# Softmax steps, rstd, weight conversion and the last batch's theta and y rearranged in a fused attention and gating kernel

## The chip, the cores and the metric

The kernel runs on one core of one Trainium2 chip. The metric is the device time of one execution in microseconds (us), as the median of several runs. The engines are named as in the profile: PE (TensorE matmul), PEld (its weight load), DVE (VectorE), ACT (ScalarE), POOL (GpSimd) and SP (SyncE, which here issues every DMA).

## What is computed

Attention with two kinds of masks (4 local heads, 4 strided heads), then a gated layer with a normalization and a mixing over tokens, then a layer with cos and sin of theta and a second mixing over tokens. B = 4, S = 576, 8 heads of 64, so d = 512. Cut to what matters:

```python
scores = where(mask, 0.125 * q @ k.T, -1e9); attn = softmax(scores)   # + 1e-9 in the divisor
x = merge_heads(attn @ v)                                   # (4, 576, 512)
h = relu(x @ w_in); u, v = h[..., :512], h[..., 512:]
v_n = (v - mean(v)) / sqrt(var(v) + 1e-6)
x2 = (u * (einsum('ts,bsd->btd', w_spatial, v_n) + b_spatial)) @ w_out
theta = x2 @ w_theta
y = einsum(w_tok_r, x2 * cos(theta)) + einsum(w_tok_i, x2 * sin(theta))
t = x2 + y
out = t + relu(t @ w_ch)
```

The weights w_in, w_out, w_theta, w_tok_r, w_tok_i and w_ch arrive as float64.

## The kernel before

Every large matmul takes a value as a pair of float16 tensors, hi and lo, and is done in three passes (`PASS`: hi·hi, lo·hi, hi·lo), each as two matmuls of 288 columns (`mm2`). The hi part is a copy (ACT as a rule), the lo part a subtraction on DVE or POOL.

**Order of the work.** Generators for the main path (`main_v`, `main_mid`, `main_end`) yield after each chunk; at each yield `others()` hands out conversion parts whose due time has come (by a count of matmul columns, `clock`) and steps of the attention of a later batch (`ATT_AT`). The Tile scheduler then sets each engine's order from priorities; `hv`, `ha` and `hg` issue with a priority raised by `AHEAD`. Each engine works its list in order. For a batch the main path is v (with the statistics and `rstd`), then u and sp (the first mixing), x (w_out), th (theta, with `z_chunk` for cos and sin), then y (the second mixing) and c (w_ch). y and c of batch b come after v of batch b+1, so that other matmuls lie between th and y; the last batch has no v behind it, and y follows th at once.

**Attention.** Batches 0 and 1 run in float32 (`attention32`, L408), 11 units each. A unit goes: scores on PE into a PSUM tile, a maximum on DVE (L395), the step that multiplies it by -0.125 (L403, DVE, 96x4 or 128x4), four Exp with sums on ACT (L405), then in `softmax_div` a step on the sums (L341, DVE), a reciprocal (L342) and a multiplication (L343); then a transpose on PE (L445), its copy out (L446, ACT), the matmul with v (L420), and the evacuation of `av` into xT (L355 on ACT, L356 on DVE). Batches 2 and 3 (`attention`, L485) use float16 pairs and the same `softmax_div` with another scale. In batch 1, `sc` and `av` have one PSUM buffer each, so that the PE waits at L445 for the evacuation L356 of an earlier unit.

**Conversion of float64 weights** (`stage`, `from_f64`, `part`, `prep_w`, `tok_part`; L189 to L258). A block of 128 rows and 512 or 576 columns is loaded as raw 64 bit words, scaled in place on ACT (L203), put together with three integer operations on DVE (L204, L205, L206), copied to float16 on ACT (L119) and subtracted on POOL (L211). There are 29 such blocks: 8 of w_in, 4 of w_out, 4 of w_theta, 9 of the token weights, 4 of w_ch. Until `switch`, the raw words lie in the two halves of `x2f` in turn and the values in quarters of `x2h`; after it, in tiles of the pools `s2` and `s1`. `WIN_AT` sets after which units of the first attention a w_in block is handed out, `CONV_*` hold due time, lead and gap of the others.

**rstd** (L527) is a chain of 15 small DVE steps on 128x5, with the copy at L592: a shift estimate and three Newton rounds.

**The end.** In `main_mid` (L694) th of column blocks 0 and 1 is done for rows 0 to 2 of x2h first, block 0 then block 1, and then row 3 of each; blocks 2 and 3 follow whole. A `z_chunk` (L673) is a chain over ACT and DVE: turns (ACT, `ta<-th`), fraction (DVE), Abs and two Sin (ACT), a product with x2f (DVE), the hi copy into vn (ACT), the lo subtraction (DVE), and then two DMA transposes from vn into zf (L686, hi and lo), after which y can use the block. `main_end` (L707) runs y of a column block over 9 row groups, in each of them the three passes.

Of the kernel before, what the change touches and what calls it, by code (L numbers as in the profile page):

```python
# [13 lines left out]
F32 = mybir.dt.float32  # L14
# [37 lines left out]
E_ZLO = 'vvvvvvvv'  # L52
WARM = 6
ATT_AT = (None, (2.7, 4.0), (74.5, 4.4), (169.9, 4.6))
WIN_AT = (0, 0, 0, 0, 1, 1, 1, 1)
CONV_SP = (20.0, 9.9, 1.9)
CONV_OUT = (37.0, 12.0, 2.5)
CONV_TH = (49.0, 12.0, 2.5)
CONV_TOK = (61.0, 10.0, 2.0)
CONV_CH = (87.0, 14.1, 2.4)  # L60
F64_SHIFT = 2.0 ** -111


# [1 line left out]
def kernel(  # L65
# [118 lines left out]

    early = [True, 0]

    xs4 = [x2h[:, e, c:c + 2, :].rearrange("p c n -> p (c n)").bitcast(F32)[:, 0:S] for e in range(2) for c in (0, 2)]

    def stage():  # L189
        if early[0]:  # L190
            i = early[1]
            early[1] += 1
            return x2f[:, i % 2 * 2:i % 2 * 2 + 2, :].rearrange("p a n -> p (a n)").bitcast(I64), xs4[i % 4]
        return s2("wstg").rearrange("p a n -> p (a n)").bitcast(I64), s1("wx")
# [18 lines left out]
    def prep_w(dst_hi, dst_lo, src, n, late=True):  # L213
        stg, x = stage()
        nc.sync.dma_start(stg[:, 0:n], src)
        part(dst_hi, dst_lo, from_f64(stg, x, n), late)

    def win_parts(half):
        c = slice(half * DM, (half + 1) * DM)
        for i in range(NC):  # L220
            yield lambda i=i: prep_w(win[:, 0, i, c], win[:, 1, i, c], w_in[i * P:(i + 1) * P, c], DM, False)

    def sq_parts(dst, src):
        for i in range(NC):
            yield lambda i=i: prep_w(dst[:, 0, i, :], dst[:, 1, i, :], src[i * P:(i + 1) * P, :], DM)

    def sp_part(i):
        stg = stage()[0].bitcast(F32).rearrange("p (a n) -> p a n", a=2)
        nc.sync.dma_start(stg, w_spT[i * P:(i + 2) * P, :].rearrange("(a p) n -> p a n", p=P))
        nc.scalar.activation(wsp[:, 0, i:i + 2, :], stg, AF.Copy, scale=SPS)  # L230
        nc.vector.scalar_tensor_tensor(wsp[:, 1, i:i + 2, :], stg, SPS, wsp[:, 0, i:i + 2, :],
                                       op0=ALU.mult, op1=ALU.subtract)

    def sp_tail():
        stg = stage()[0].bitcast(F32).rearrange("p (a n) -> p a n", a=2)
# [12 lines left out]
    def tok_part(i):  # L248

        stg, x = stage()  # L250
        r = 0
        while r < P:
            g = i * P + r
            w, k = (w_tr, g) if g < S else (w_ti, g - S)
            n = min(P - r, S - k)
            nc.sync.dma_start(stg[r:r + n, 0:S], w[k:k + n, :])
            r += n
        part(wtok[:, 0, i, :], wtok[:, 1, i, :], from_f64(stg, x, S), True)  # L258


    SOFF = [0, 126, 252, 378, 448]
# [130 lines left out]
    def softmax32(sc, sm, st, R, way):  # L392
        X = mybir.AxisListType.X
        mx = st[0:R, 0, :]
        nc.vector.tensor_reduce(out=mx.rearrange("p (i j) -> p i j", i=2), in_=sc[0:R], op=ALU.max, axis=X)  # L395
        smv = sm[0:R].rearrange("p (i j) k -> p i j k", i=2)
        if way == "d":
            nc.vector.tensor_tensor(smv, sc[0:R], mx.rearrange("p (i j) -> p i j", i=2).unsqueeze(3).broadcast_to(
                [R, 2, 2, P]), ALU.subtract)
            nc.scalar.activation(sm[0:R], sm[0:R], AF.Exp, scale=0.125)  # L400
            nc.vector.tensor_reduce(out=st[0:R, 2, :], in_=sm[0:R], op=ALU.add, axis=X)
        else:
            nc.vector.tensor_scalar(st[0:R, 1, :], mx, -0.125, None, op0=ALU.mult)  # L403
# [123 lines left out]
    def rstd(st, n, rows):  # L527
        r = slice(0, rows)
        a, y, t = st[r, 0, 0:n], st[r, 1, 0:n], st[r, 2, 0:n]
        hv.tensor_scalar(a, a, 1e-6, None, op0=ALU.add)  # L530
        hv.tensor_scalar(t.bitcast(I32), a.bitcast(I32), 1, None, op0=ALU.logical_shift_right)
        hv.tensor_scalar(y.bitcast(I32), t.bitcast(I32), -1, 0x5F3759DF, op0=ALU.mult, op1=ALU.add)
        hv.tensor_scalar(a, a, -0.5, None, op0=ALU.mult)
# [21 lines left out]
    def main_v(b):  # L555
# [25 lines left out]
        for pr in V_ORDER:  # L581
# [31 lines left out]
    def main_mid(b):  # L613
# [93 lines left out]
    def main_end(b):  # L707
# [17 lines left out]

# [36 lines left out]
    timed([lambda i=i: tok_part(i) for i in range(NZ)], *CONV_TOK)  # L762
# [131 lines left out]
```

## Time and profile before

| | us |
|---|---|
| runs before: median of 3 | 539.72 |
| lowest, highest | 536.95, 546.14 |
| the profiled execution, its own time | 538.83 |
| span of its trace | 536.8 |

The trace covers the first to the last instruction of the profiled execution; 2.0 us lie around it. PE is busy for 485.4 us of the span (90%), DVE for 366.2, ACT for 306.9, POOL for 96.1. Matmuls are pipelined and their ends are modelled, so that small gaps on the PE do not show. The granted clock of the PE is given as a share of its full 2.4 GHz; 0.5 is 1.2 GHz. In a row of the timeline, the bracket gives the idle time before the instruction and what ended it.

### The profile page before, as it was taken

How to read it: one execution, taken by the hardware profiler on the slowest of the kernel's cores; microseconds unless marked ns; L12 is line 12 of the kernel's file. 1: busy time of each engine (PE TensorE's matmuls, PEld its weight loads, DVE VectorE, ACT ScalarE, POOL GpSimd, SP SyncE). 2: the span in 40 equal slices, each digit the busy share in tenths (PEclk: the TensorE clock that was granted, in tenths of full speed). 3: DMA queues.
4: the chain of work that ended last, by engine and by line, in shares of the span. 5: the costliest groups of instructions: out<-in, count | busy, mean ns of one | idle time of the engine just before them, and what ended most of it. 6: DMA issues, size and time to landing. Idle time of an engine off the chain costs nothing. (4 is left out here: it accounts for less than half of the span.)

```text
span 536.8 us, 10338 instructions
## 1 busy us (share of the span) xinstructions
PE 485.4 (90%) x4019; PEld 365.7 (68%) x4019; DVE 366.2 (68%) x817; ACT 306.9 (57%) x737; POOL 96.1 (18%) x72
## 2 busy tenths in 40 slices
PE   6777978777887998999899998999999999996996
PEld 6764556555653776777666876777747777774775
DVE  1788999999987998898558778874389121227212
ACT  1777787667798436777585457764582121158101
POOL 0021134543300542001000400010003300100110
PEclk9789999999898998999999999999999999998999
DMA  8666577454159514755529034522082020004402
GB/s 278 239 232 189 162 262 219 161 152 139 37 98 244 136 40 108 194 135 143 137 40 137 1 81 127 148 45 37 1 150 27 1 89 1 1 2 91 86 1 88
DMA packets 75861, 59.88 MB, mean 112 GB/s; under 512 B 59939, under 2 KB 60963, under 8 KB 75813
## 3 DMA queue, kind: packets, MB, share of 16 engines
q1 hardware_dynamic: 75812, 59.23, 42.2%
q8 instruction: 31, 0.51, 0.4%
q14 instruction: 18, 0.14, 0.1%
HBM read 40.08 MB, written 4.72 MB: 83 GB/s over the span
## 5 line engine op out<-in xcount | busy, mean ns | idle before, releaser
L517 PE MATMUL y<-wtok,zf 128*128 128x288 f16 x864 | 108.8, 288 | 4.1 <-DMA zf<-vn 4.1
L517 PEld LDWEIGHTS <-zf 128*128 128x128 f16 x864 | 84.6, 99 | 27.7 <-DMA zf<-vn 4.7
L517 PE MATMUL sp<-wsp,vn 128*128 128x288 f16 x384 | 50.8, 286 | 2.1 <-ACT vn L108 1.6
L517 PE MATMUL c<-x2h,wch 128*128 128x288 f16 x384 | 49.6, 289 | 1.6 <-ACT o L108 1.6
L517 PE MATMUL x<-zf,wout 128*128 128x288 f16 x384 | 49.7, 288 | 0.0
L517 PE MATMUL th<-x2h,wth 128*128 128x288 f16 x384 | 49.6, 290 | 0.0
L517 PE MATMUL u<-xT,win 128*128 128x288 f16 x384 | 49.5, 286 | 0.0
L517 PEld LDWEIGHTS <-vn 128*128 128x128 f16 x416 | 40.3, 98 | 12.3 <-ACT vn L108 1.8
L578 PE MATMUL v<-win,xT 128*128 128x512 f16 x192 | 44.9, 387 | 3.0 <-DVE xT L356 1.9
L108 POOL TENSOR_TENSOR x2h<-x2f,x2h 128x576 f16<-128x576 f32 x20 | 27.6, 1381 | 110.4 <-DVE x2h L108 42.5
L517 PEld LDWEIGHTS <-wch 128*128 128x128 f16 x384 | 37.8, 99 | 11.7 <-issue 2.0
L517 PEld LDWEIGHTS <-wth 128*128 128x128 f16 x384 | 38.1, 100 | 10.3 <-issue 0.2
L517 PEld LDWEIGHTS <-wout 128*128 128x128 f16 x384 | 37.2, 98 | 9.5
L517 PEld LDWEIGHTS <-win 128*128 128x128 f16 x384 | 37.2, 98 | 9.1
L336 ACT ACTIVATE sm<-sm,st 96x128 f32<-96x128 f32 (+1 forms) x88 | 34.2, 390 | 7.8 <-DVE st L332 7.7
L578 PEld LDWEIGHTS <-xT 128*128 128x128 f16 x192 | 18.8, 99 | 25.3 <-DVE xT L356 2.6
L108 ACT ACTIVATE x2h<-x2f 128x576 f16<-128x576 f32 x24 | 16.5, 686 | 30.4 <-DVE x2f L108 30.0
L108 DVE SCALAR_TENSOR_TENSOR x2f<-y,x2f 128x576 f32<-128x576 f32 x16 | 12.0, 752 | 28.5 <-PE y L517 28.5
L108 POOL TENSOR_TENSOR zf<-u,zf 128x576 f16<-128x576 f32 x8 | 10.3, 1287 | 106.5 <-ACT zf L108 106.5
L108 DVE TENSOR_TENSOR ta<-ta,x2f 128x1152 f32<-128x1152 f32 x16 | 21.5, 1352 | 8.9 <-ACT ta L108 8.9
L108 ACT ACTIVATE o<-c 128x576 f32<-128x576 f32 (+1 forms) x17 | 10.3, 613 | 30.3 <-PE c L517 30.0
L343 DVE TENSOR_TENSOR sm<-sm,st 96x512 f32<-96x512 f32 (+1 forms) x33 | 26.7, 809 | 0.8
(122 smaller groups left out, 890.2 us busy)
## 6 DMA issues: line engine op xcount, KB each, us to landing
qs<-in_qd_dram SPq DMA_DIRECT2D x16, 288.0 KB, 3.0
out_dram<-o SPq DMA_DIRECT2D x15, 288.0 KB, 2.1
x2f<-in_w_in_dram SPq DMA_DIRECT2D x8, 512.0 KB, 5.3
ks<-in_kl_dram SPq DMA_DIRECT2D x8, 304.0 KB, 3.1
k<-in_kzs_dram SPq DMA_DIRECT2D x4, 576.0 KB, 5.4
wstg<-in_w_tr_dram SPq DMA_DIRECT2D x4, 576.0 KB, 4.7
wstg<-in_w_ti_dram SPq DMA_DIRECT2D x4, 576.0 KB, 4.7
ks<-in_ks_dram SPq DMA_DIRECT2D x8, 288.0 KB, 3.2
```

Source lines behind the costliest of these rows:

```text
L108: return f(*args, **kwargs)
L336: nc.scalar.activation(sm[0:R, n, :], sm[0:R, n, :], AF.Exp, bias=st[0:R, 1, n:n + 1], scale=-1.0, accum_out=st[0:R, 2, n:n + 1])
L343: N[eng].tensor_tensor(sm[0:R], sm[0:R], st[0:R, 3, :].unsqueeze(2).broadcast_to([R, 4, P]), ALU.mult)
L517: nc.tensor.matmul(ps, lhs, rhs, **kw)
L578: nc.tensor.matmul(ps, xh[:, xe, c, i * P:(i + 1) * P], win[:, we, c, DM:2 * DM], start=(c == 0 and n == 0), stop=(c == NC - 1 and n == 2))
```

## The change

Four parts.

1. **Softmax steps.** In the attention of batches 0 and 1 the step on the maximum (L403 before) and the step on the sums (L341 before) become ACT activations (Copy with scale, or with scale and bias). Batches 2 and 3 keep theirs on DVE.
2. **rstd** takes the variance where it stands, with scale and constant folded in: 12 steps for 15.
3. **Conversion.** A pass converts two row blocks at once: 15 passes for 29 blocks (14 of two blocks, one of one). The raw words lie in the whole of `x2f`, in a part of `zf`, and later in `xT[0]`; the values in a half of `x2h` or in an `s2` tile. The gaps of `CONV_*` are doubled, and `WIN_AT` hands out one w_in pass after the fifth and one after the seventh step of the first attention.
4. **Last batch.** th runs block 0 rows 0 to 2, block 1 row 0, block 0 row 3, block 1 rows 1 to 3. y of column block 0 runs all nine row groups with the hi half of z (two passes each) and then all nine with the lo half.

```diff
-WIN_AT = (0, 0, 0, 0, 1, 1, 1, 1)
+WIN_AT = (0, 0, 0, 0, 1, 0, 1, 0)
...
-CONV_TOK = (61.0, 10.0, 2.0)
+CONV_TOK = (61.0, 10.0, 4.0)
...
+    raw0 = x2f.rearrange("p c n -> p (c n)").bitcast(I64)
+    raw1 = zf[:, 0:8 * S].bitcast(I64)
+    raw2 = xT[0].rearrange("p e c n -> p (e c n)").bitcast(I64)
+    vals = [x2h[:, e].rearrange("p c n -> p (c n)").bitcast(F32) for e in range(2)]
+
+    def stage(late_raw=None):
+        i = early[1]
+        early[1] += 1
         if early[0]:
...
+            return (raw0, raw1)[i % 2], vals[i % 2]
+        return late_raw, s2("wx").rearrange("p a n -> p (a n)")
...
+    def pair(ap, n):
+        return ap[:, 0:2 * n].rearrange("p (a n) -> p a n", a=2)
+
+    def prep_w(dst, src, c, i, late=True):
+        stg, x = stage(raw2)
+        n = c.stop - c.start
+        nc.sync.dma_start(pair(stg, n), src[i * P:(i + 2) * P, c].rearrange("(a p) n -> p a n", p=P))
+        x = pair(from_f64(stg, x, 2 * n), n)
+        part(dst[:, 0, i:i + 2, c], dst[:, 1, i:i + 2, c], x, late)
...
     def softmax_div(eng, sm, st, R, scale):
-        nc.vector.tensor_scalar(st[0:R, 3, :], st[0:R, 2, :], 1e-9, 1.0 / scale, op0=ALU.add, op1=ALU.mult)
+        if scale == XS:
+            nc.scalar.activation(st[0:R, 3, :], st[0:R, 2, :], AF.Copy, bias=1e-9 / scale, scale=1.0 / scale)
+        else:
+            nc.vector.tensor_scalar(st[0:R, 3, :], st[0:R, 2, :], 1e-9, 1.0 / scale, op0=ALU.add, op1=ALU.mult)
...
-            nc.vector.tensor_scalar(st[0:R, 1, :], mx, -0.125, None, op0=ALU.mult)
+            nc.scalar.activation(st[0:R, 1, :], mx, AF.Copy, scale=-0.125)
...
+    def rstd(st, var, n):
...
+        h, y, t = st[:, 0, 0:n], st[:, 1, 0:n], st[:, 2, 0:n]
+        hv.tensor_scalar(h, var, 1e-6, 0.5 / VNS ** 2, op0=ALU.add, op1=ALU.mult)
+        hv.tensor_scalar(t.bitcast(I32), h.bitcast(I32), 1, None, op0=ALU.logical_shift_right)
+        hv.tensor_scalar(y.bitcast(I32), t.bitcast(I32), -1, 0x5EF759DF - 2 ** 31, op0=ALU.mult, op1=ALU.add)
         for it in range(3):
...
-        for cs in ((0, 1, 2), (3,)):
-            for m in range(2):
-                th_mm(m, tiles[m], cs)
-                if cs[0] == 3:
-                    z_chunk(m, tiles[m])
-                yield
+        order = ((0, (0, 1, 2)), (1, (0, 1, 2)), (0, (3,)), (1, (3,)))
+        if b == B - 1:
+            order = ((0, (0, 1, 2)), (1, (0,)), (0, (3,)), (1, (1, 2, 3)))
+        for m, cs in order:
+            th_mm(m, tiles[m], cs)
+            if cs[-1] == 3:
+                z_chunk(m, tiles[m])
+            yield
...
+            rounds = [(i, PASS) for i in range(NZ)]
+            if m == 0 and b == B - 1:
+
+                rounds = [(i, ((0, 0), (0, 1))) for i in range(NZ)] + [(i, ((1, 0),)) for i in range(NZ)]
+            for k, (i, passes) in enumerate(rounds):
+                for n, (ze, we) in enumerate(passes):
                     mm2(ps, zz[:, i, ze, m * P:(m + 1) * P], wtok[:, we, i, :],
```

The first instructions of ACT, before (L203 is the scaling of the first w_in block, which waits for its DMA; L405 are the Exp):

```order
L316 ACTIVATE maskb<-mask 128x512
L203 ACTIVATE x2f<-x2f 128x512
L405 ACTIVATE smx,st<-at,st 96x128 x8
L119 ACTIVATE win<-x2h 128x512
L405 ACTIVATE smx,st<-at,st 96x128 x3
```

And in the changed kernel (L418 is the step on the maximum, L354 that on the sums, L207 the scaling of a w_in pass, L420 the Exp):

```order
L328 ACTIVATE maskb<-mask 128x512
L418 ACTIVATE st<-st 96x4
L420 ACTIVATE smx,st<-at,st 96x128 x4
L418 ACTIVATE st<-st 96x4
L207 ACTIVATE x2f<-x2f 128x1024
L420 ACTIVATE smx,st<-at,st 96x128 x4
L354 ACTIVATE st<-st 96x4
```

The Exp of the first unit now stand ahead of the first scaling, those of the second still behind it, and the scaling has twice the columns.

POOL in batch 0, before (L211 are the subtractions of the conversion, L108 those of the main path):

```order
L211 TENSOR_TENSOR win<-x2h,win 128x512 x8
L211 TENSOR_TENSOR wout<-x2h,wout 128x512
L108 COPY k_92<-vn 64x512
L108 TENSOR_TENSOR vn<-vr_636,vn 128x2x512
L211 TENSOR_TENSOR wout<-x2h,wout 128x512 x3
L211 TENSOR_TENSOR wth<-x2h,wth 128x512
L108 TENSOR_TENSOR zf<-u_766,zf 128x576
L211 TENSOR_TENSOR wth<-x2h,wth 128x512
```

And in the changed kernel (L215 for L211):

```order
L215 TENSOR_TENSOR win<-x2h,win 128x2x512 x4
L215 TENSOR_TENSOR wout<-x2h,wout 128x1024 x2
L108 COPY k_92<-vn 64x512
L108 TENSOR_TENSOR vn<-vr_608,vn 128x2x512
L215 TENSOR_TENSOR wth<-x2h,wth 128x1024 x2
L108 TENSOR_TENSOR zf<-u_735,zf 128x576
```

There are half as many subtractions, each of two blocks, and both of w_theta now stand ahead of the first of the main path's zf.

DVE in the last batch's z, before (ta0 to ta3 are the four column blocks; `ta<-th` is the fraction, `ta<-ta,x2f` the product, `vn<-ta,vn` the lo subtraction):

```order
L108 SCALAR_TENSOR_TENSOR ta0_5565<-th0_5521,ta0_5565 128x576
L108 SCALAR_TENSOR_TENSOR ta1_5582<-th1_5522,ta1_5582 128x576
L108 TENSOR_TENSOR ta0_5565<-ta0_5565,x2f_99 128x1152
L108 SCALAR_TENSOR_TENSOR ta2_5618<-th2_5593,ta2_5618 128x576
L108 TENSOR_TENSOR vn_97<-ta0_5565,vn_97 128x1152
L108 TENSOR_TENSOR ta1_5582<-ta1_5582,x2f_99 128x1152
```

And in the changed kernel:

```order
L108 SCALAR_TENSOR_TENSOR ta0_5428<-th0_5396,ta0_5428 128x576
L108 TENSOR_TENSOR ta0_5428<-ta0_5428,x2f_99 128x1152
L108 SCALAR_TENSOR_TENSOR ta1_5457<-th1_5397,ta1_5457 128x576
L108 TENSOR_TENSOR vn_97<-ta0_5428,vn_97 128x1152
L108 SCALAR_TENSOR_TENSOR ta2_5493<-th2_5468,ta2_5493 128x576
L108 TENSOR_TENSOR ta1_5457<-ta1_5457,x2f_99 128x1152
```

The product of block 0 comes ahead of the fraction of block 1, and the lo subtraction of block 0 ahead of the fraction of block 2.

## Rows read from the trace of the kernel before

**Rows 1.** Windows of stages: us, then busy time (x instructions) of each engine, clock, DMA.

```profile
20.00:60.00 40.00, 33.40 (x257) 22.84 (x256) 34.17 (x82) 29.71 (x99) 8.44 (x7) 0.94 0.63 202
60.00:110.00 50.00, 41.19 (x349) 31.14 (x348) 48.66 (x104) 37.73 (x99) 19.06 (x13) 1.00 0.58 186
110.00:153.00 43.00, 34.78 (x277) 26.53 (x276) 39.55 (x64) 31.82 (x80) 15.69 (x11) 0.96 0.39 115
208.80:475.90 267.10, 263.15 (x2303) 199.92 (x2303) 164.85 (x418) 146.09 (x340) 30.33 (x22) 0.99 0.35 78
```

**Rows 2.** The chain that ended last, near the end: start us, us, what.

```profile
476.21 5.16 PE th L517 x42
481.37 0.02 issue
481.40 0.66 ACT ta L108
...
486.71 1.06 ACT vn L108
...
489.23 3.22 DMA zf<-vn
```

**Rows 3.** Timeline, 470 to 537 us, all engines.

```profile
476.05 11.92 PE L517 MATMUL th<-x2h,wth 128*128 128x288 f16 x96
...
484.97 1.36 DVE L108 TENSOR_TENSOR ta<-ta,x2f 128x1152 f32<-128x1152 f32 x1 [1.39 <-ACT ta L108]
...
491.18 0.42 PE L517 MATMUL y<-wtok,zf 128*128 128x288 f16 x2 [3.20 <-DMA zf<-vn]
...
492.50 27.86 PE L517 MATMUL y<-wtok,zf 128*128 128x288 f16 x214 [0.91 <-DMA zf<-vn]
```

**Rows 4.** Windows of 10 us, columns as in rows 1.

```profile
210.00:220.00 10.00, 10.00 (x90) 7.69 (x89) 7.59 (x30) 6.56 (x21) 0.00 (x0) 0.89 0.41 124
...
250.00:260.00 10.00, 8.36 (x86) 6.49 (x86) 8.74 (x15) 7.98 (x22) 0.80 (x1) 1.00 0.76 177
...
490.00:500.00 10.00, 7.92 (x52) 5.55 (x53) 7.61 (x7) 5.87 (x8) 0.00 (x0) 0.83 0.90 172
```

**Rows 5.** Groups of DVE instructions by form, 0 to 153 us: busy us, mean ns.

```profile
L205 DVE SCALAR_TENSOR_TENSOR x2h<-x2f,x2h 128x512 int32<-128x512 int32 x16 | 13.2, 828 | 1.9 <-ACT x2f L203 1.8
...
L343 DVE TENSOR_TENSOR sm<-sm,st 128x512 f32<-128x512 f32 x5 | 6.1, 1221 | 0.0
...
L341 DVE TENSOR_SCALAR st<-st 96x4 f32<-96x4 f32 x12 | 4.1, 339 | 0.0
...
L341 DVE TENSOR_SCALAR st<-st 128x4 f32<-128x4 f32 x10 | 3.7, 368 | 0.2
...
L403 DVE TENSOR_SCALAR st<-st 128x4 f32<-128x4 f32 x9 | 2.4, 272 | 0.0
...
L403 DVE TENSOR_SCALAR st<-st 96x4 f32<-96x4 f32 x11 | 1.7, 156 | 0.0
```

**Rows 6.** Timeline of DVE, 0 to 100 us.

```profile
28.48 0.16 DVE L403 TENSOR_SCALAR st<-st 96x4 f32<-96x4 f32 x1
28.55 0.16 DVE L341 TENSOR_SCALAR st<-st 96x4 f32<-96x4 f32 x1
28.62 0.42 DVE L204 TENSOR_SCALAR x2h<-x2f 128x512 int32<-128x512 int32 x1
...
37.35 0.68 DVE L206 SCALAR_TENSOR_TENSOR x2h<-x2f,x2h 128x512 int32<-128x512 int32 x1
...
80.57 2.10 DVE L341 TENSOR_SCALAR st<-st 96x4 f32<-96x4 f32 x1
```

**Rows 7.** Timelines: POOL from 78 us, then POOL and DVE from 194 us.

```profile
78.10 4.54 POOL L108 TENSOR_TENSOR vn<-vr,vn 128x1024 f16<-128x1024 f32 x1 [1.65 <-ACT vn L108]
82.60 1.15 POOL L211 TENSOR_TENSOR wout<-x2h,wout 128x512 f16<-128x512 f32 x1
...
194.29 2.90 POOL L108 TENSOR_TENSOR vn<-vr,vn 128x1024 f16<-128x1024 f32 x1 [1.25 <-ACT vn L108]
195.12 2.35 DVE L204 TENSOR_SCALAR wx<-wstg 128x512 int32<-128x512 int32 x1
```

**Rows 8.** Timelines of ACT and PE, start of the kernel, and one small ACT copy.

```profile
14.12 0.67 ACT L203 ACTIVATE x2f<-x2f 128x512 f32<-128x512 f32 x1 [8.14 <-DMA x2f<-in_w_in_dram]
...
16.26 0.58 PE L383 MATMUL at<-maskb,identb 128*96 128x128 bf16 x4 [4.43 <-ACT smx L405]
...
46.52 0.23 ACT L355 ACTIVATE xT<-av 128x72 f16<-128x72 f32 x1
46.65 0.36 ACT L405 ACTIVATE smx<-at,st 128x128 f32<-128x128 f32 x1
```

More of the change, by code (lines that the diff above doesn't have):

```diff
@@ L54 @@
 ATT_AT = (None, (2.7, 4.0), (74.5, 4.4), (169.9, 4.6))
-WIN_AT = (0, 0, 0, 0, 1, 1, 1, 1)
+WIN_AT = (0, 0, 0, 0, 1, 0, 1, 0)
 CONV_SP = (20.0, 9.9, 1.9)
-CONV_OUT = (37.0, 12.0, 2.5)
-CONV_TH = (49.0, 12.0, 2.5)
-CONV_TOK = (61.0, 10.0, 2.0)
-CONV_CH = (87.0, 14.1, 2.4)
+CONV_OUT = (37.0, 12.0, 5.0)
+CONV_TH = (49.0, 12.0, 5.0)
+CONV_TOK = (61.0, 10.0, 4.0)
+CONV_CH = (87.0, 14.1, 4.8)
 F64_SHIFT = 2.0 ** -111
@@ L185 @@
     early = [True, 0]
-    xs4 = [x2h[:, e, c:c + 2, :].rearrange("p c n -> p (c n)").bitcast(F32)[:, 0:S] for e in range(2) for c in (0, 2)]
-    def stage():
+    raw0 = x2f.rearrange("p c n -> p (c n)").bitcast(I64)
[5 more added lines that the diff above has]
+        early[1] += 1
         if early[0]:
[L191 to L194, printed above, removed]
+            return (raw0, raw1)[i % 2], vals[i % 2]
+        return late_raw, s2("wx").rearrange("p a n -> p (a n)")
     def from_f64(stg, x, n):
@@ L211, in part @@
         N[E_WLO[late]].tensor_tensor(dst_lo, x, dst_hi, ALU.subtract)
[L213 to L216, printed above, removed]
+    def pair(ap, n):
[6 more added lines that the diff above has]
+        part(dst[:, 0, i:i + 2, c], dst[:, 1, i:i + 2, c], x, late)
     def win_parts(half):
         c = slice(half * DM, (half + 1) * DM)
-        for i in range(NC):
-            yield lambda i=i: prep_w(win[:, 0, i, c], win[:, 1, i, c], w_in[i * P:(i + 1) * P, c], DM, False)
+        for i in range(0, NC, 2):
+            yield lambda i=i: prep_w(win, w_in, c, i, False)
     def sq_parts(dst, src):
-        for i in range(NC):
-            yield lambda i=i: prep_w(dst[:, 0, i, :], dst[:, 1, i, :], src[i * P:(i + 1) * P, :], DM)
+        for i in range(0, NC, 2):
+            yield lambda i=i: prep_w(dst, src, slice(0, DM), i)
     def sp_part(i):
-        stg = stage()[0].bitcast(F32).rearrange("p (a n) -> p a n", a=2)
+        stg = pair(stage()[0].bitcast(F32), S)
         nc.sync.dma_start(stg, w_spT[i * P:(i + 2) * P, :].rearrange("(a p) n -> p a n", p=P))
@@ L234, in sp_tail @@
     def sp_tail():
-        stg = stage()[0].bitcast(F32).rearrange("p (a n) -> p a n", a=2)
+        stg = pair(stage()[0].bitcast(F32), S)
         for j in range(2):
@@ L246, in sp_tail, with tok_part @@
                                        op0=ALU.mult, op1=ALU.subtract)
[L248 to L258, printed above, removed]
+    def tok_part(i, raw):
+        stg, x = stage(raw)
+        m = min(2, NZ - i)
+        for a in range(m):
+            r = 0
+            while r < P:
+                g = (i + a) * P + r
+                w, k = (w_tr, g) if g < S else (w_ti, g - S)
+                n = min(P - r, S - k)
+                nc.sync.dma_start(stg[r:r + n, a * S:(a + 1) * S], w[k:k + n, :])
+                r += n
+        x = from_f64(stg, x, m * S).rearrange("p (a n) -> p a n", a=m)
+        part(wtok[:, 0, i:i + m, :], wtok[:, 1, i:i + m, :], x, True)
     SOFF = [0, 126, 252, 378, 448]
@@ L525, in split @@
         lo_eng.tensor_tensor(dst[1], srcf, dst[0], ALU.subtract)
[L527 to L533, printed above, removed]
+    def rstd(st, var, n):
[3 more added lines that the diff above has]
+        hv.tensor_scalar(y.bitcast(I32), t.bitcast(I32), -1, 0x5EF759DF - 2 ** 31, op0=ALU.mult, op1=ALU.add)
         for it in range(3):
             hv.tensor_tensor(t, y, y, ALU.mult)
-            hv.tensor_tensor(t, t, a, ALU.mult)
-            hv.scalar_tensor_tensor(y, t, 1.5, y, op0=ALU.add, op1=ALU.mult)
-        hv.tensor_scalar(y, y, VNS, None, op0=ALU.mult)
+            hv.tensor_tensor(t, t, h, ALU.mult)
+            hv.scalar_tensor_tensor(y, t, 1.5, y, op0=ALU.subtract, op1=ALU.mult)
     def tail_mm(ps, x, w, cols):
@@ L591, in main_v @@
             v_relu(pr, ps)
-        hv.tensor_copy(rs[:, 0, 0:5], mv[:, :, 1])
-        rstd(rs, 5, P)
+        rstd(rs, mv[:, :, 1], 5)
         for q in range(3):
@@ L715, in main_end @@
             ps = pm(f"y{m}")
-            for i in range(NZ):
-                for n, (ze, we) in enumerate(PASS):
+            rounds = [(i, PASS) for i in range(NZ)]
[3 more added lines that the diff above has]
+                for n, (ze, we) in enumerate(passes):
                     mm2(ps, zz[:, i, ze, m * P:(m + 1) * P], wtok[:, we, i, :],
-                        i == 0 and n == 0, i == NZ - 1 and n == 2)
-                if i == NZ - 1:
+                        k == 0 and n == 0, k == len(rounds) - 1 and n == len(passes) - 1)
+                if k == len(rounds) - 1:
                     tok_evac(m, ps)
-                if i % 3 == 2:
+                if k % 3 == 2:
                     yield
@@ L761 @@
     timed(list(sq_parts(wth, w_th)) + [switch], *CONV_TH)
-    timed([lambda i=i: tok_part(i) for i in range(NZ)], *CONV_TOK)
+    timed([lambda i=i: tok_part(i, (raw2, raw1)[i // 2 % 2]) for i in range(0, NZ, 2)], *CONV_TOK)
     timed(sq_parts(wch, w_ch), *CONV_CH)
```

## The prediction

> **What bounds the kernel now.** I read the windows by stage first. From 208.8 to 475.9 us PE is busy for 263.2 of 267.1 us [rows 1]: nothing that DVE or ACT saves there can move the end, and the L341 steps of batches 2 and 3, which stay on DVE, lie in it. Two places are left. From 20 to 153 us PE works 33.4 + 41.2 + 34.8 = 109.4 of 133 us, while DVE is busy for 34.2 + 48.7 + 39.6 = 122.4, or 92% [rows 1]; this is where the attention of batches 0 and 1, the main path of batch 0 and the weight conversion meet, and DVE is the engine that everything passes through. ACT has 99.3 of the 133 us. The second place is the step from theta to y in the last batch: the chain that ended last leaves PE at 481.37 after 42 theta matmuls, runs through ACT and DVE to the hi copy that ends at 487.77, then through a DMA transpose [rows 2]. PE itself has theta work until 476.05 + 11.92 = 487.97, waits 3.20 us, does two matmuls of y, waits 0.91 more for the lo transpose, and runs y without a stop from 492.50 [rows 3].
>
> **The last batch.** A theta matmul takes 5.16 / 42 = 0.123 us [rows 2]. Block 0 was complete after 18 + 18 + 6 = 42 of them and is now after 18 + 6 + 6 = 30, so its z chain starts 12 x 0.123 = 1.47 us earlier, at 479.9 for 481.40. From there to the end of the product the steps are the same (484.97 + 1.36 - 481.40 = 4.93 us [rows 2, 3]), which gives 484.9; then the hi copy stood until 486.71 behind a step of block 1 [rows 2], which starts later now, so it gains another 0.3. The hi copy ends near 486.0, 1.75 us earlier. The step from there to the first y matmul (491.18 - 487.77 = 3.4 us) is the transpose, and stays: y starts at 489.4. Its first 36 matmuls (4.4 us) now need the hi half alone, so the lo transpose, which was there 1.3 us after the hi one, has time: the 0.91 us stop goes. What is late next is block 1, whose hi and lo are needed 54 matmuls (6.6 us) after the start; by the same steps I place their landing at about the same 496, so up to 0.5 us may come back there.
>
> Before, y ran its last 214 matmuls in 27.86 us, 1.5 more than 214 x 0.123: the granted clock was 0.83 of 2.4 GHz in the window from 490 to 500 us, after the stop [rows 4], that is, part of it at 1.2 GHz. Now the stop is 1.5 us (487.97 to 489.4). A window with 1.64 us of idle PE, 250 to 260, kept 1.00; but from 210 to 220 the clock averaged 0.89 though PE never stopped in it [rows 4], so a short stop excludes nothing. With full clock y ends at 489.4 + 216 x 0.123 = 516.0 for 520.36, a gain of 4.3; with the same fall it is 2.8. I take 3.9. Below, 2.3 (block 1 late as well).
>
> **The small steps.** 42 leave DVE: 22 of L341 and 20 of L403 [rows 5]. Where nothing blocks it, such a step takes 0.07 us from its start to the next one's [rows 6], so 42 x 0.07 = 2.9 us. On ACT they come back. The nearest row is a copy of 72 columns, 0.23 us long, with the next instruction 0.13 behind its start [rows 8]: 42 x 0.13 = 5.5 us, 9.7 at the full 0.23. ACT has 133 - 99.3 = 33.7 us free from 20 to 153, and each step comes between instructions of the same unit that were on ACT anyway. I cost it at nothing; if that cover is gone the bound is the 9.7, less what the conversion frees on ACT. A gain is possible too, since a unit's chain no longer queues behind DVE for these steps.
>
> **Conversion.** 29 blocks become 15 passes, so 14 x 3 = 42 instructions leave DVE; the columns stay. What goes is the fixed part of an instruction, for which the 0.07 of a step on 4 columns is the nearest row: 2.9 us (0 to 2.9). rstd loses 3 steps of at most 0.16 us [rows 6], 0.5 us in batch 0; in the other batches other matmuls lie over it. Together DVE sheds 2.9 + 2.9 + 0.5 = 6.3 us.
>
> Against this stands POOL. A step of 96x4 that takes 0.16 us took 2.10 at 80.57, until 82.67; POOL's subtraction ended at 82.64 [rows 6, 7]. A 512 column L204 that takes 0.42 took 2.35 at 195.12, until 197.47, while a 1024 column subtraction ran to 197.19 [rows 6, 7]. So some DVE instructions stand still until POOL's instruction is over. In the six groups of rows 5 the time above count x the shortest (0.68 for L205 and L343, as L206 in rows 6, 0.16 for the small steps) is 2.3 + 2.7 + 2.2 + 2.1 + 1.0 + 0 = 10.3 us, over 29 subtractions of mostly 1.2 to 1.5 us (1.15 at its shortest [rows 7]). Half of it sat on the steps that leave, but the POOL instruction is still there and the next sensitive DVE instruction meets it. A pass now subtracts 1024 or 1152 columns, at least 2 x 1.15 = 2.3 us in one piece. The blocked time of a pass lies between 0 (DVE is at work on something that does not mind) and 1.93 (the L204 above); twice what a block had is 0.7. I take 0.9, since the longer piece outlasts more of the instructions that do not mind: 15 x 0.9 = 13.5, which is 3.2 more than before.
>
> The Trainium skill, page "SBUF — State Buffer", section "Who interferes with whom", says that VectorE and GpSimd share a port pair as an exclusive lock: a VectorE instruction with two SBUF inputs, or in a two-port mode, waits for the whole GpSimd instruction, while one that reads PSUM alone or reduces does not. Read strictly, it speaks against passes of double length; the rows agree as to the wait, and its full effect is the third case below.
>
> **Raw loads.** The first ACT scaling waited until 14.12 for its block, and the Exp of all units behind it, so that PE stood 4.43 us until 16.26 [rows 8]. Now a pass is 1 MB for 0.5 and lands later, by 0.5 MB at the 202 GB/s to which the nearest stage comes [rows 1], 2.5 us; but the Exp of the first unit go ahead of it in that idle time. I take 0, with 1.5 either way. On SP the loads of two token row groups now wait for xT[0] to be free, with loads of q and k queued behind; these serve units that come tens of us later, so 0, with up to 2 if that cover is short.
>
> **Sum.** DVE -6.3 + 3.2 = -3.1, counted in full as DVE is 92% busy; last batch -3.9. The profiled execution took 538.83 (span 536.8 and 2.0 around it): 538.8 - 7.0 = 531.8. The median of the runs is 0.9 above it, so I forecast 532.5 for the runs.
>
> **The rivals.**
> - *The blocked time goes with the steps.* If the 5.3 us on L341 and L403 disappear and merged passes block no more than the rest, DVE sheds 6.3 + 5.3 = 11.6, and the last batch 3.9 or more: 538.8 - 15.5 + 0.9 = 524.2. For it: L342 and the maximum are next in those chains, and short. Against: L205 and L343 wait as often.
> - *Long subtractions hold DVE.* Each of the 15 passes blocks it for the 1.93 us of the L204 row: 29.0 for 10.3, so +18.7 - 6.3 - 3.9 = +8.5, or 548.2, slower than before. It decides from (10.3 + 6.3 + 3.9) / 15 = 1.37 us a pass. For it: DVE has nearly always something queued. Against: the blocked time before was far below POOL's own.
> - *The last batch does not do what it says.* y starts no earlier, because the lo half or block 1 comes late and the clock falls again: -3.1 alone, 536.6.
>
> **How the numbers follow.** Forecast 0.54, with its own range 528 to 537; first rival 0.21, second 0.12, third 0.13. The range 522 to 543 leaves out the second rival's centre and the outer edge of the first. Two per cent, about what a measurement of this kernel can tell from no change, is 528.9 and 550.5. The first rival and a sixth of the forecast lie below: 0.30. Of the second rival a third lies above 550.5: 0.04. The rest is 0.66.
>
> **What would show it.** The first y matmul of the last batch 1.5 us behind the last theta matmul and no second stop; clock 1.00 behind it. The end of y 4 us closer to the end of theta. DVE groups of the conversion at twice the columns with means above twice the old shortest ones, and long L358 or L208 to L210 that end with a POOL subtraction. The stage from 20 to 153 us about 3 us shorter. If y of batch 0 begins over 8 us earlier, or later at all, the forecast's stage term is wrong.

## The result and the profile after

The changed kernel took 533.68 us (median of 6 runs, 531.33 to 535.84), the kernel before 543.86 in the same comparison (6 runs, 536.95 to 546.14): a ratio of 0.985, 95% interval 0.981 to 0.989. Runs over 1.5% above the fastest of their kernel count as disturbed and stay out of a ratio, here 545.64 and 546.14 of before, so that it is not the quotient of the two medians. Measured once more in a later comparison it was 532.40 us and 0.985 [0.981, 0.988], with before at 541.33. The profiled execution took 533.31 us, 5.5 less than the one of before, which had been among the quicker of its kernel.

The windows by stage, of the kernel after, with the columns of [rows 1]:

```profile
20.00:60.00 40.00, 32.43 (x249) 22.34 (x248) 34.02 (x58) 31.77 (x112) 8.72 (x4) 0.94 0.65 214
60.00:110.00 50.00, 40.48 (x322) 29.79 (x321) 46.32 (x71) 34.23 (x87) 15.51 (x7) 0.97 0.53 174
110.00:153.00 43.00, 37.43 (x305) 28.37 (x304) 36.00 (x48) 35.29 (x92) 18.30 (x7) 0.96 0.43 140
208.80:475.90 267.10, 262.38 (x2300) 199.29 (x2299) 163.01 (x404) 145.85 (x338) 29.56 (x22) 1.00 0.34 77
```

From 20 to 153 us DVE is busy for 34.02 + 46.32 + 36.00 = 116.3 us, 6.1 less than before, and ACT for 101.3, 2.0 more. The long stage of batches 1 to 3 is unchanged. The end, first the chain that ended last (start us, us, what), then PE on the timeline, both of the kernel after:

```profile
475.05 3.69 PE th L532 x30
478.74 0.02 issue
478.76 0.66 ACT ta L108
...
483.72 1.17 ACT vn L108
...
484.95 3.32 DMA zf<-vn
```

```profile
474.88 11.92 PE L532 MATMUL th<-x2h,wth 128*128 128x288 f16 x96
...
488.32 26.63 PE L532 MATMUL y<-wtok,zf 128*128 128x288 f16 x216 [1.52 <-DMA zf<-vn]
```

Against [rows 2, 3]: the chain leaves PE after 30 theta matmuls, y waits 1.52 us for its first transpose instead of 3.20, the second stop is gone, and 216 matmuls run in one piece. The windows at the end of the kernel after keep the full clock, where 490 to 500 us had 0.83 [rows 4]:

```profile
480.00:490.00 10.00, 8.48 (x70) 6.55 (x69) 6.28 (x7) 8.84 (x14) 0.00 (x0) 1.00 0.31 59
490.00:500.00 10.00, 10.00 (x84) 7.98 (x83) 7.61 (x7) 4.88 (x7) 1.27 (x1) 1.00 0.91 144
```

From the start of the last theta to the end of y it is 514.95 - 474.88 = 40.07 us, before 44.31: 4.2 us gained here. Only 1.2 us of the span were gained ahead of 475 us, and where DVE now stands still shows in its groups by form, 0 to 153 us, of the kernel after (busy us, mean ns):

```profile
L358 DVE TENSOR_TENSOR sm<-sm,st 96x512 f32<-96x512 f32 x6 | 7.7, 1291 | 0.1
L358 DVE TENSOR_TENSOR sm<-sm,st 128x512 f32<-128x512 f32 x5 | 6.7, 1345 | 0.2
L209 DVE SCALAR_TENSOR_TENSOR x2h<-x2f,x2h 128x1024 int32<-128x1024 int32 x4 | 5.7, 1422 | 0.0
...
L209 DVE SCALAR_TENSOR_TENSOR wx<-zf,wx 128x1152 int32<-128x1152 int32 x2 | 3.8, 1888 | 0.0
...
L357 DVE RECIPROCAL st<-st 96x4 f32<-96x4 f32 x12 | 1.9, 162 | 1.7 <-ACT st L354 1.7
```

The softmax's multiplication L358, 0.68 us where nothing holds it, now has means of 1.29 and 1.35. For each group of DVE's instructions of one line, tile and form I took the time above count x the shortest one of that profile, and added it up over all groups from 0 to 150 us: 22.6 us before, 18.6 after (the expectations below say 22.3 and 19.0). I call it DVE's time above the shortest.

### The profile page after: what moved, and what is told of

Same layout as the page of the kernel before. It is cut to its first block, busy times and chain, and to the rows that moved or that the text cites. A ratio compares the mean times of both kernels' runs of the same rounds, so it can differ in the third digit from the quotient of the medians.

```text
span 531.5 us, 10195 instructions
## 1 busy us (share of the span) xinstructions
PE 481.9 (91%) x4019; PEld 362.3 (68%) x4019; DVE 357.2 (67%) x721; ACT 309.8 (58%) x751; POOL 92.8 (17%) x58
## 5 line engine op out<-in xcount | busy, mean ns | idle before, releaser
L108 POOL TENSOR_TENSOR x2h<-x2f,x2h 128x576 f16<-128x576 f32 x20 | 27.0, 1349 | 109.9 <-DVE x2h L108 47.6
L592 PE MATMUL v<-win,xT 128*128 128x512 f16 x192 | 43.5, 379 | 1.6 <-ACT xT L370 1.4
L532 PEld LDWEIGHTS <-wth 128*128 128x128 f16 x384 | 37.7, 99 | 10.3 <-issue 0.5
L108 POOL TENSOR_TENSOR zf<-u,zf 128x576 f16<-128x576 f32 x8 | 14.0, 1746 | 112.1 <-ACT zf L108 112.1
L108 ACT ACTIVATE x2h<-x2f 128x576 f16<-128x576 f32 x24 | 16.4, 685 | 28.8 <-DVE x2f L108 28.4
L358 DVE TENSOR_TENSOR sm<-sm,st 96x512 f32<-96x512 f32 (+1 forms) x33 | 29.6, 897 | 0.9
L108 DVE SCALAR_TENSOR_TENSOR x2f<-y,x2f 128x576 f32<-128x576 f32 x16 | 12.0, 753 | 26.5 <-PE y L532 26.4
L108 DVE TENSOR_TENSOR ta<-ta,x2f 128x1152 f32<-128x1152 f32 x16 | 21.6, 1353 | 9.7 <-ACT ta L108 9.7
L108 ACT ACTIVATE o<-c 128x576 f32<-128x576 f32 (+1 forms) x17 | 10.3, 613 | 29.9 <-PE c L532 29.7
```

The source lines that it names most:

```text
L108: return f(*args, **kwargs)
L532: nc.tensor.matmul(ps, lhs, rhs, **kw)
L592: nc.tensor.matmul(ps, xh[:, xe, c, i * P:(i + 1) * P], win[:, we, c, DM:2 * DM], start=(c == 0 and n == 0), stop=(c == NC - 1 and n == 2))
```

## The experiments

In the table, *u1* is where u of batch 1 starts in the profiled execution and *tail* the time from the last theta's start to the end of y. The two clocks are the granted clock of TensorE from 8 to 64 us and from 64 to 220 us. Times are medians of 5 to 33 runs. Ratios, with their 95% interval, are to the kernel before as it was measured beside each (median 543.9 in the first comparison, 541.3 to 541.8 in the others).

| kernel | us | ratio | u1 | clock 8-64 | clock 64-220 | tail |
|---|---|---|---|---|---|---|
| before | 541.6 | 1 | 219.6 | 0.91 | 0.97 | 44.3 |
| last batch alone | 537.3 | 0.992 [0.989, 0.995] | 222.7 | 0.91 | 0.95 | 40.0 |
| conversions alone | 546.2 | 1.009 [1.006, 1.012] | 225.6 | 0.82 | 0.96 | 44.2 |
| softmax steps alone | 540.3 | 0.998 [0.995, 1.002] | 220.3 | 0.94 | 0.93 | 45.4 |
| change without last batch | 536.9 | 0.993 [0.990, 0.996] | 215.6 | 0.94 | 0.98 | 44.5 |
| change without softmax steps | 545.6 | 1.007 [1.005, 1.010] | 227.2 | 0.82 | 0.92 | 40.1 |
| change without rstd | 536.9 | 0.992 [0.989, 0.996] | 215.9 | 0.91 | 0.97 | 41.0 |
| change, first profile | 533.7 | 0.985 [0.981, 0.989] | 218.3 | 0.91 | 0.97 | 40.1 |
| change, second profile | 532.4 | 0.985 [0.981, 0.988] | 219.1 | 0.91 | 0.95 | 40.1 |
| change, first weights in single blocks | 534.0 | 0.987 [0.983, 0.991] | 218.4 | 0.88 | 0.96 | 40.1 |
| change, GpSimd split | 528.3 | 0.978 [0.973, 0.982] | 215.4 | 0.94 | 0.98 | 40.1 |
| change, GpSimd and VectorE split | 531.4 | 0.980 [0.976, 0.984] | 216.9 | 0.91 | 0.95 | 40.1 |
| conversions alone, VectorE split | 546.1 | 1.009 [1.006, 1.012] | 226.8 | 0.85 | 0.93 | 45.4 |
| conversions alone, GpSimd split | 540.1 | 0.997 [0.995, 1.000] | 220.9 | 0.79 | 0.98 | 44.1 |

From u1 to the last theta all of them need 255 to 258 us. So but for these 3 us, all that tells the profiles apart happens ahead of u1 or in the tail. One profile's u1 is no fine measure, though. Before and "last batch alone" run the same instructions in the same order on every engine ahead of 220 us, and so do the change, in both its profiles, and the change without the last batch; yet u1 differs by 3.1 us in the first group and by 3.5 in the second.

**The last batch, alone and left out.** The first kernel is before with

```diff
+        if b == B - 1:
+            order = ((0, (0, 1, 2)), (1, (0,)), (0, (3,)), (1, (1, 2, 3)))
...
+            if m == 0 and b == B - 1:
+                rounds = [(i, ((0, 0), (0, 1))) for i in range(NZ)] + [(i, ((1, 0),)) for i in range(NZ)]
```

> Part 4 alone (theta and y of the last batch reordered, all else as before). Theory: it gives its whole gain at the end of the program, 4.2 us as between the two profiled kernels (from th begin to y end 45.4 us there become 40.1, less what th itself began earlier): ratio to before about 0.992. The stretch from the end of batch 3's theta to y shows y 1.5 us behind, no second stop of TensorE and a granted clock of 1.00 in the 10 us around it; everything ahead of 470 us stays as before within 1 us. Rival (the last batch gains nothing): ratio 1.000, y begins as late as before or the third product's matmuls take the time back.

Measured: 0.992 [0.989, 0.995], 4.3 us. The tail went from 44.3 us (476.05 to 520.36; the 45.4 of the expectation is not before's) to 40.0. The stretch ahead of 470 us did not stay within 1 us in this profile: u1 came 3.1 us later and the last theta 2.7, with a clock of 0.95 for 0.97, in a program that is the same up to there. The second is the whole change with these lines undone.

> The whole change without part 4. Theory: the parts add up, so this is 4 us slower than the whole change, about 537.7 us, and the difference stands between 475 us and the end: y again 3 us behind and a second stop of 0.9 us. What is left against before is parts 1 to 3: 1.3 us by the two profiles, up to 6 us by the medians (ratio 0.989 to 0.998). Rival (the gain is that of parts 1 to 3 and the last batch gives nothing): 533.7 us, ratio 0.982.

Measured: 536.9 us, 3.2 to 4.5 more than the change. PE in the timeline of the change without it:

```profile
471.82 11.92 PE L532 MATMUL th<-x2h,wth 128*128 128x288 f16 x96
...
486.94 0.42 PE L532 MATMUL y<-wtok,zf 128*128 128x288 f16 x2 [3.20 <-DMA zf<-vn]
...
488.27 28.06 PE L532 MATMUL y<-wtok,zf 128*128 128x288 f16 x214 [0.91 <-DMA zf<-vn]
```

The old 3.20, the second stop and the slower 214 matmuls are back. Both ways part 4 is worth about 4 us, and it adds to whatever the rest does: the tail is 40.0 to 40.1 us in seven of the eight profiles of the table that carry it (41.0 in the eighth, without rstd's change) and 44.1 to 45.4 in the six others. The rival that it gains nothing falls.

**Conversions alone.** Before with the diff's parts around `stage`, `prep_w`, `tok_part` and the tables of due times, in short

```diff
-        for i in range(NC):
+        for i in range(0, NC, 2):
-            yield lambda i=i: prep_w(dst[:, 0, i, :], dst[:, 1, i, :], src[i * P:(i + 1) * P, :], DM)
+            yield lambda i=i: prep_w(dst, src, slice(0, DM), i)
```

> Conversions two row blocks a pass, alone. Theory: 42 instructions fewer on VectorE save about 2.9 us of it between 20 and 153 us, its first load is twice as large and TensorE's first long stop, 4.43 us at 16 us before, grows to about 6 as in the whole change; net between -1 and +1 us, ratio 0.998 to 1.002. Rival (the long subtractions on GpSimd hold VectorE 1.93 us each, the second rival of the prediction): +15 us, ratio 1.028. Rival (the passes are what made the kernel faster, all of the rest of the gain): -5 us, ratio 0.991.

Measured: slower by 0.9%, 5 us, outside what any of the three gave. DVE's busy time from 8 to 220 us fell from 188.1 to 184.3 us all the same.

**Softmax steps alone.** Before with

```diff
-        nc.vector.tensor_scalar(st[0:R, 3, :], st[0:R, 2, :], 1e-9, 1.0 / scale, op0=ALU.add, op1=ALU.mult)
+            nc.scalar.activation(st[0:R, 3, :], st[0:R, 2, :], AF.Copy, bias=1e-9 / scale, scale=1.0 / scale)
...
-            nc.vector.tensor_scalar(st[0:R, 1, :], mx, -0.125, None, op0=ALU.mult)
+            nc.scalar.activation(st[0:R, 1, :], mx, AF.Copy, scale=-0.125)
```

> The two small softmax steps on ScalarE, alone. Theory: 42 steps fewer on VectorE save 2.9 us between 20 and 153 us, of which one to three reach the end: ratio 0.994 to 0.998. Rival (the time that GpSimd holds VectorE goes with the steps, the first rival of the prediction): -8 us, ratio 0.985, and VectorE's time above each form's shortest, 22.3 us before, falls under 15. Rival (the steps now wait in ScalarE's line behind its long instructions and the chain of a softmax gets longer): slower, ratio above 1.003.

Measured: 0.998 [0.995, 1.002], 1 us that can't be told from none. DVE's time above the shortest fell from 22.7 to 17.1 us (0 to 160 us): part of the blocked time does go with the steps, as the first rival said, but nearly none of it reaches the end. The edit does more than move the steps: from 20 us on PE runs its matmuls in another order than before. The two effects were not taken apart.

**The change without the softmax steps.** The same lines undone in the changed kernel.

> The whole change without the two softmax steps on ScalarE. Theory: VectorE gets 2.9 us back between 20 and 153 us, the kernel is 1 to 3 us slower than the changed one (ratio 1.002 to 1.006). Rival (the steps are the greater part of the gain, since they open places where GpSimd doesn't hold VectorE): 5 us or more slower, ratio 1.010. Rival (ScalarE's line costs what VectorE gains): no difference, ratio 0.999 to 1.001.

Measured: 1.007, 13 us slower than the change, far beyond the 5 of the rival, and 12 us more than these steps gave alone. The parts do not add up. In this kernel's timeline, POOL, then DVE, then PE:

```profile
50.45 2.68 POOL L215 TENSOR_TENSOR win<-x2h,win 128x1024 f16<-128x1024 f32 x1 [11.99 <-ACT win L119]
```

```profile
49.92 1.22 DVE L209 SCALAR_TENSOR_TENSOR x2h<-zf,x2h 128x1024 int32<-128x1024 int32 x1
...
51.20 0.17 DVE L354 RECIPROCAL st<-st 128x4 f32<-128x4 f32 x1
51.29 2.92 DVE L210 SCALAR_TENSOR_TENSOR x2h<-zf,x2h 128x1024 int32<-128x1024 int32 x1
54.13 0.41 DVE L368 TENSOR_TENSOR xT<-av,xT 128x252 f16<-128x252 f32 x1
54.46 0.68 DVE L355 TENSOR_TENSOR smx<-smx,st 128x512 f32<-128x512 f32 x1
```

```profile
28.96 0.52 PE L457 MATMUL sc<-ident,smx 96*128 96x96 f32 x4 [1.40 <-DVE smx L355]
...
55.28 0.63 PE L457 MATMUL sc<-ident,smx 128*128 128x128 f32 x4 [3.13 <-DVE smx L355]
```

A conversion instruction (L210) stood until POOL's subtraction was over at 53.13, the multiplication of the softmax, whose reciprocal had been ready at 51.37, came behind it, and PE had nothing for 3.13 us. The windows of this kernel and of the changed one show what came with such stops:

```profile
30.00:40.00 10.00, 8.41 (x50) 7.06 (x52) 8.92 (x17) 7.29 (x27) 2.13 (x1) 0.50 0.71 263
50.00:60.00 10.00, 5.90 (x41) 4.19 (x40) 7.83 (x10) 5.59 (x9) 4.81 (x2) 0.87 0.54 188
```

```profile
30.00:40.00 10.00, 7.47 (x62) 6.23 (x61) 8.38 (x15) 7.52 (x31) 2.12 (x1) 0.83 0.78 270
50.00:60.00 10.00, 7.80 (x52) 4.25 (x52) 6.80 (x10) 5.68 (x17) 2.76 (x2) 1.00 0.45 145
```

Without the steps on ACT the granted clock was 0.50 (1.2 of 2.4 GHz) for all of 30 to 40 us, after the stop of 1.40 at 28.96. In the changed kernel the stretch kept 0.83, and 50 to 60 us 1.00, with 1.25 us as PE's longest stop in them. The order of the work on PE and ACT differs between the two kernels here too.

**Whose length costs: VectorE's instructions or GpSimd's.** Conversions alone, with one of the two issued for each row block again (the columns and everything else as in the merged pass):

```diff
+        k = n // 2 if n > S else n
+        for r in range(0, n, k):
+            f = slice(r, r + k)
+            nc.vector.tensor_scalar(xi[:, f], lo[:, f], 29, None, op0=ALU.logical_shift_right)
...
```

> The conversions alone (two row blocks a load and a pass on ScalarE and GpSimd), but VectorE's three instructions of a pass issued for each row block, as before. The conversions alone were 1.0093 of before. Theory A (the softmax's small steps stand in VectorE's line behind conversion instructions of 1.2 us instead of 0.68): the loss goes, ratio 0.998 to 1.002. Theory B (the loss comes of GpSimd's long subtractions, or of the larger first load): it stays, ratio 1.006 to 1.012.

```diff
-        N[E_WLO[late]].tensor_tensor(dst_lo, x, dst_hi, ALU.subtract)
+        for a in range(x.shape[1]):
+            N[E_WLO[late]].tensor_tensor(dst_lo[:, a], x[:, a], dst_hi[:, a], ALU.subtract)
```

> The conversions alone, but GpSimd's subtraction of a pass issued for each row block, as before. Theory B (long subtractions hold VectorE; in the whole change the split was worth 4 us): the ratio falls from 1.0093 to about 1.002. Theory A (VectorE's line of longer conversion instructions): it stays at 1.006 to 1.012. If both splits help in part, both are true in part.

Measured: splitting VectorE's changes nothing (1.009), splitting GpSimd's takes all of the loss away and a little more (0.997, 6.1 us). Theory A falls, and of theory B the half that blames GpSimd's subtractions holds; the larger first load stands in both kernels. In the traces GpSimd's split leaves the order of DVE, ACT and PE ahead of 220 us exactly as it was, here and in the change, so that GpSimd's shorter instructions are all that differs. VectorE's split changes the order on PE from 13 us on and is the less clean test. The next kernels have the same splits in the whole change; beside them ran the change itself once more, which gave the second median above.

> The changed kernel once more, as the mark for the two beside it: 531 to 536 us, ratio to before 0.981 to 0.990.

> The changed kernel with each low part of a converted pass subtracted in two instructions, one for each row block, as before. Theory: how long one subtraction on GpSimd is decides nothing; VectorE's time above each form's shortest between 0 and 150 us, 19.0 us in the changed kernel, stays within 2 us and the time within 1 us (ratio to the changed kernel 0.998 to 1.002). Rival (a long subtraction holds VectorE for its whole length): that time falls by 4 us or more, most of it on the multiplication of the softmax (96 and 128 x 512), and the kernel is 2 to 4 us faster, ratio 0.993 to 0.996.

> The whole change with GpSimd's subtraction and VectorE's three instructions of a pass issued for each row block. Against the change with GpSimd's alone split (0.9775 of before). Theory A (with the small steps off VectorE its longer instructions hurt nobody): 0.976 to 0.982, no better, since 42 instructions of VectorE come back with about 0.07 us each. If the length of VectorE's instructions still costs: 0.970 to 0.975, the fastest of all.

Measured: with GpSimd's split 528.26 us (527.29 to 531.93), 4.1 less than the changed kernel beside it and 2.2% under before [0.973, 0.982]: the fastest of all, the changed kernel with the two-line edit above. With VectorE's split as well 531.4: no gain from shorter VectorE instructions here either, again with another order of the work. The groups by form of the kernel with GpSimd's split, 0 to 153 us:

```profile
L216 POOL TENSOR_TENSOR wtok<-wx,wtok 128x576 f16<-128x576 f32 x9 | 13.5, 1522 | 17.4 <-ACT wtok L119 17.4
...
L108 POOL TENSOR_TENSOR zf<-u,zf 128x576 f16<-128x576 f32 x2 | 2.7, 1366 | 5.1 <-ACT zf L108 5.1
```

```profile
L359 DVE TENSOR_TENSOR sm<-sm,st 96x512 f32<-96x512 f32 x6 | 7.9, 1310 | 0.1
L359 DVE TENSOR_TENSOR sm<-sm,st 128x512 f32<-128x512 f32 x5 | 5.5, 1102 | 0.2
...
L359 DVE TENSOR_TENSOR smx<-smx,st 128x512 f32<-128x512 f32 x5 | 4.2, 846 | 0.0
```

and POOL's of the changed kernel:

```profile
L215 POOL TENSOR_TENSOR wtok<-wx,wtok 128x1152 f16<-128x1152 f32 x4 | 10.6, 2647 | 13.4 <-ACT wtok L119 13.4
...
L108 POOL TENSOR_TENSOR zf<-u,zf 128x576 f16<-128x576 f32 x2 | 6.2, 3106 | 6.6 <-ACT zf L108 6.6
```

The multiplications on 128 rows lose 0.2 us each, those on 96 none. In all, DVE's time above the shortest falls from 18.6 and 20.9 us (the two profiles of the change, 0 to 160 us) to 17.2, which is less than the 4 us that the rival asked for and little more than those two differ by. PE's stop at 55 us, 3.13 us in the conversions alone as in the kernel above, is 2.79 with the split. So it is shown that the length of GpSimd's instruction costs these 4 to 6 us; that all of them pass through held VectorE instructions is not. POOL's own subtraction of u, 1.37 us here as the mean of two, took 3.11 in the change, but that is no effect of the split: in the second profile of the change it took 1.35.

**The start.** The changed kernel with the first two row blocks of the projection's weights loaded and converted one at a time (`WIN_AT` hands out the extra pass):

```diff
+        if half == 1:
+            for i in range(2):
+                yield lambda i=i: first_w(i, c)
+        for i in range(2 * half, NC, 2):
```

> The changed kernel with the first pass of the projection's weights again as two passes of one row block, each with a load of half the size. Theory: the first conversion gets its weights about 2 us earlier (14.1 us for 16.2), and TensorE's first long stop, 5.92 us, falls to about 4.4 and is over 2 us earlier. If the time lost there reaches the end, the kernel is 1 to 2 us faster than the changed one (ratio 0.996 to 0.998). Rival (the start is hidden: a later wait ends at the same time whatever the start does): within 0.5 us, with the first x of batch 0 no earlier than 115 us.

Measured: 534.0 beside 532.4 us, which the intervals do not tell apart. PE at the start of the changed kernel, then of this one:

```profile
18.80 0.58 PE L398 MATMUL at<-maskb,identb 128*96 128x256 bf16 x2 [5.92 <-ACT smx L420]
```

```profile
16.13 0.58 PE L408 MATMUL at<-maskb,identb 128*96 128x128 bf16 x4 [4.72 <-ACT smx L430]
```

The stop is 1.2 us shorter and ends 2.7 us earlier (16.13 for 18.80), about as expected, but x of batch 0 starts at 115.5 as in the change (115.6). The earlier start is lost by then, with a lower clock on the way (0.88 for 0.91).

**The reciprocal square root.** The changed kernel with the former steps:

```diff
-        rstd(rs, mv[:, :, 1], 5)
+        hv.tensor_copy(rs[:, 0, 0:5], mv[:, :, 1])
+        rstd(rs, 5, P)
```

> The whole change with the former 16 steps of the reciprocal square root. Forecast of the prediction: 0.5 us slower than the changed kernel, ratio to before 0.984 to 0.987. Rival (the four parts don't add up, and this one is faster without the new steps by as much as the other three together miss): 0.976 to 0.982.

Measured: without the new rstd 536.9 us, but its 11 runs lie between 531.7 and 541.5, ten us apart, and its profiled execution (531.7) was the fastest of them. Neither the 0.5 us nor the rival is borne out. The kernel is slower than the change by 3.2 to 4.5 us in the median, with intervals that just touch. So small an edit (12 steps for 15; the expectation's 16 is a miscount) does not only take steps away: from about 73 us on PE runs in another order than in the change, ACT from 79 us and POOL from 108. Whether the steps or the order cost the time is open. The same edit alone on before wasn't tried.

## Why the prediction was right, and where not

The forecast of 532.5 us is 1.2 below the first median and 0.1 above the second. So near a hit is in part luck: the forecast set out from a median of 539.7 for before, from three runs, where 33 give 541.6, and it forecast 7 us of gain where 0.985 is 8. From 541.6 the same sum would have given 534.6. Its two sums stand up as sums: -3.9 for the last batch (measured 4.3 alone, 4.2 in the profiles), and -3.1 for the other three parts together (0.993, that is -3.9 with -5.5 to -2.3). Below the sums it was less good.

- *The last batch* went step by step as worked out: the hi copy ended at 484.89, with a theta that began 1.17 us earlier than before's, which is 486.06 on the prediction's scale for its 486.0; y 1.5 us behind theta, no second stop, clock 1.00. The clock was the open half of the term; the 4.3 us end of the range was right.
- *Blocked by POOL, +3.2 us.* The mechanism was right and its size a little small: the split is worth 4.1 us in the change and 6.1 in the conversions alone, and DVE's time above the shortest, 17.1 us with the softmax steps alone, is 18.6 and 20.9 with the passes added. (The 10.3 us that the term was worked out from stand in 0 to 153 us, where only 25 of the 29 subtractions lie, so a block had 0.41 us and not 0.36.) The second rival's 18.7 us was far off: only some of POOL's long subtractions met an instruction that minds. One of the changed kernel that did, POOL's row and DVE's:

```profile
48.29 2.35 POOL L215 TENSOR_TENSOR win<-x2h,win 128x1024 f16<-128x1024 f32 x1 [13.98 <-ACT win L119]
```

```profile
48.70 2.48 DVE L358 TENSOR_TENSOR smx<-smx,st 128x512 f32<-128x512 f32 x1
```

The multiplication, 0.68 us alone, ended 0.54 us after the subtraction did. The Trainium skill, page "SBUF — State Buffer", section "Who interferes with whom", adds that the order of issue decides who blocks, so that GpSimd can be the one that waits. The trace agrees that GpSimd can wait, in the first profile of the change, POOL's row and DVE's:

```profile
110.71 4.42 POOL L108 TENSOR_TENSOR zf<-u,zf 128x576 f16<-128x576 f32 x1 [4.61 <-ACT zf L108]
```

```profile
110.77 0.68 DVE L358 TENSOR_TENSOR sm<-sm,st 96x512 f32<-96x512 f32 x1
111.37 1.34 DVE L210 SCALAR_TENSOR_TENSOR wx<-xT,wx 128x1152 int32<-128x1152 int32 x1
112.64 1.34 DVE L210 SCALAR_TENSOR_TENSOR wx<-zf,wx 128x1152 int32<-128x1152 int32 x1
```

Three of DVE's ran at full speed, and POOL's, 1.27 us in the second profile, ended 1.15 us after the last of them. That the order of issue decides it was not tried.
- *"Counted in full as DVE is 92% busy"* is the step that failed. From 20 to 153 us DVE shed 6.1 us, twice the 3.1 forecast, since the blocked time went down with the steps where I had it go up; and it did not come out as time: the three parts gave 3.9 us. The conversions alone took 3.8 us off DVE and lost 5 us; the softmax steps alone took 6.3 off it (188.1 to 181.8, 8 to 220 us) and gained 1. Nor do the prices of the parts, which I added up, hold in company. Alone, steps and conversions were -1 and +5. With each other, in the change without rstd, they come to about nothing, as its 0.992 is what the last batch gives alone. They reach -4 only with the new rstd beside them; and conversions with the new rstd, without the steps, lose about 8 (1.007 with the last batch in it). Each of these figures is uncertain by some 2 us.
- *The first rival* was half true. The blocked time does go with the steps, by 5.6 us when they move alone, and this is worth 1 us there, if anything. Beside the conversions with the old rstd they are worth about 5 (from +5 to nothing), in the change 13, so it is not the double passes alone that make the 13.
- *Raw loads at nothing:* the first conversion came 2 us later (16.23 for 14.12) and PE stood 5.92 for 4.43 us, and still the term holds, since the earlier start gained nothing.
- *The small steps on ACT* were hidden, as taken: alone they made nothing slower (0.998), and ACT's busy time from 20 to 153 us grew by 2.0 us.

So the total was right partly because two errors cancelled: the conversions were worse than taken, the softmax steps better in the company of the rest.

What joins them is shown only in part. Of the prediction's signs, y of batch 0 began 3.5 and 2.8 us earlier in the two profiles (169.9 and 170.6 for 173.4), as forecast; but in "last batch alone", the same program as before up to there, it began at 176.1. The order in which u1 comes over the 14 profiles follows the clock: the time lost to it, (1 - clock) x window for the two windows of the table, is 6.5 us in the two kernels that reach u1 first and 22.6 in the last, and over all of them 1 us more lost goes with 0.8 us later (correlation 0.90). Part of this is scatter between executions: within each of the two groups of the same program, too, the later u1 has the lower clock. If the stops bring the low clock about, each one avoided counts twice, for itself and for the slow stretch behind it. That was not tried by itself; the rows only show what came after what, as at 28.96 above.

## What to carry to other kernels

Where GpSimd and VectorE work side by side, keep GpSimd's instructions short: merging them saves issue time on an engine that is busy for a fifth of the span, and lengthens what VectorE, with the softmax's multiplication, may have to wait for (splitting them was worth 4 to 6 us here). Don't add up edits to an engine by its busy time when what sets the end is a chain that passes through it: measure each part alone and left out, since here the one differs from the other by 12 us. And see in the traces whether an edit changed the order of the work: only where the order stayed, as with GpSimd's split, does a difference belong to the edited instructions alone.

## What the runs showed that I had not expected

The spread of a kernel's own runs goes with the clock. Over 33 runs of the kernel before, from 536.3 to 545.3 us, 0.01 more of the mean granted clock went with 3.1 us less (correlation -0.89; the clock from 0.956 to 0.981). A profiled execution is one draw of this: two of the same changed kernel differ by 2.3 us in their span (531.5 and 533.8). So the 1.2 us that the two profiles of the result show ahead of 475 us is no measure of parts 1 to 3, for which the medians give 3.9.

A step on 4 columns costs ScalarE 0.10 us from its start to the next one's, less than the 0.13 taken from a copy of 72 columns (rows of the changed kernel):

```profile
18.62 0.22 ACT L354 ACTIVATE st<-st 96x4 f32<-96x4 f32 x1
18.72 0.22 ACT L418 ACTIVATE st<-st 96x4 f32<-96x4 f32 x1
18.81 0.22 ACT L354 ACTIVATE st<-st 96x4 f32<-96x4 f32 x1
```
